# A chunked attention state, computed by heads right behind y

## The chip, the cores and the metric

The kernel runs on one core of one Trainium2 chip. The metric is the device time of one execution in microseconds (us), as the median of several runs.

## The reference

A recurrent attention with decay feeds a two-layer network:

```python
B, H, S, D = 4, 8, 768, 64
gamma = 1.0 - 2.0 ** (-5.0 - np.arange(H))
for t in range(S):
    state = gamma[None, :, None, None] * state + np.einsum('bhd,bhe->bhde', k[:, :, t], v[:, :, t])
    y[:, :, t] = scale * np.einsum('bhd,bhde->bhe', q[:, :, t], state)

x = y.transpose(0, 2, 1, 3).reshape(3072, 512)
h = x @ w_in                                   # 512 -> 2048
g = 0.5 * h * (1.0 + np.tanh(c * (h + 0.044715 * h * h * h)))
out = g @ w_out                                # 2048 -> 512
```

Inputs and output are float32. The kernel works in float16 with float32 sums.

## The kernel before, in words

The sequence is cut into six chunks of 128 positions; a chunk holds all four batches `b` and eight heads. A head has 64 dimensions, so heads go in four pairs `hp`, and `j` (0 or 1) is the head in its pair.

For each chunk `c` and batch `b` the attention has these steps. q and k are scaled by powers of gamma and cast to float16 (`prep1` and `prep_blk`, on GpSimd from chunk 2 on, L195 and L206), and their transposed form is made (for chunks 2 to 5 by DVE, `tr`, L263). `mm_A` (L273) multiplies k and q within the chunk, and DVE masks the product on its way out of PSUM (`ev_A`, L286). `mm_yc` (L295) multiplies the state of the earlier chunks with q, four matmuls of 128 columns; `mm_yi` (L308) adds the masked product times v, eight matmuls, each of one head: 64 weight columns, whose result goes to one half of the output partitions. `ev_Y` casts y to float16 as `xT`, the input of the network. Last, `mm_s` (L327) forms S, the sum over the chunk of k times v: four matmuls, one for each pair of heads, of 128 weight columns and 128 moving columns. Such a product holds the 64x64 blocks of the two heads on its diagonal and two mixed blocks that nothing reads. `ev_S` (L344) has DVE add the diagonal blocks to the decayed state `stg` into `st`, and `decay` (L353) has GpSimd scale `st` into `stg` for the next chunk.

The network runs on TensorE for each chunk: `moe1` (L434) with w_in, 16 blocks of hidden units, ScalarE's gelu (L449), then `moe2` (L479) with w_out, for each batch 16 matmuls of 512 columns in four units of four.

The order on every engine is the order of the program text; there is no scheduler. `run(units, after)` calls the units one by one and after unit `i` the attention steps listed for it. So the attention of chunk c+1 stands between the matmuls of the network of chunk c. For chunk 2 this is a run over the 16 `moe2` units of chunk 1: A behind units 3 and 7, y behind unit 11 (`att_Y`), and S of batch 0 to 3 behind units 12 to 15 (`att_S`: matmuls, DVE's adds, decay). Chunks 3, 4 and 5 have the same list, moved by 15 in a run of 16 `moe1` and 16 `moe2` units.

PSUM has eight banks in three pools: "h" and "o" with two each and "att" with four, taken in turn. A batch's A takes two banks of "att", y of batches 2 and 3 one each, and each S one.

Loads of q and k for chunks 2 to 5 in a blocked layout (L110), and of k and v (L98), go through SyncE's queue; v of chunk 2 alone is loaded and cast by GpSimd's queue (L670), in this kernel as in the changed one. Outputs go out mostly by GpSimd's queue (L506).

Of the kernel before, what the change touches and what calls it, by code (L numbers as in the profile page):

```python
# [12 lines left out]
ALU = mybir.AluOpType  # L13
# [3 lines left out]
def kernel(  # L17
# [9 lines left out]
    nc = tc.nc  # L27
    B, H, S, Dh = q.shape
    C = 128
    NCk = S // C  # L30
    NHP = H // 2
# [26 lines left out]
    att = ctx.enter_context(tc.tile_pool(name="att", bufs=4))  # L58
    xp = ctx.enter_context(tc.tile_pool(name="xp", bufs=2))
    gp = ctx.enter_context(tc.tile_pool(name="gp", bufs=2))  # L60
    op = ctx.enter_context(tc.tile_pool(name="op", bufs=4))
# [81 lines left out]
    for j in range(2):  # L143
# [3 lines left out]
        out=iden,  # L147
# [8 lines left out]
        out=mask.rearrange("p j hp t -> p (j hp) t"),  # L156
# [8 lines left out]
        out=misc[:, 0:1], in_=zero[:, 0:1], func=AF.Gelu_apprx_tanh, scale=1.0  # L165
# [10 lines left out]
    st = const.tile([128, NHP, B, 128], F16, name="st")  # L176
    nc.vector.memset(st, 0.0)
    stg = const.tile([128, NHP, B, 128], F32, name="stg")

    h16 = {}  # L180
# [39 lines left out]
    pss = {}  # L220
# [11 lines left out]
    def bank(tag, dt=F32, shape=(128, NHP, 128), name="ps"):  # L232
        return psum.tile(list(shape), dt, tag=tag, bufs=BANKS[tag], name=name)
# [24 lines left out]
    def ev_T(c, b, eng=nc.vector):  # L258
        copy_on(eng, qkT_tile(c, b), pss.pop(("T", c, b)))
# [29 lines left out]
    def mm_yc(c, b, tag):  # L289
        y_ps = pss["Y", c, b] = bank(tag, name="y_ps")  # L290
        if c == 0:
            return

        for hp in range(NHP):
            nc.tensor.matmul(  # L295
                out=y_ps[:, hp],
                lhsT=st[:, hp, b],
                rhs=qkT[c, b][:, 0, hp],
                start=(hp == 0),
                stop=False,  # L300
                skip_group_check=True,
            )

    def mm_yi(c, b):
        y_ps = pss["Y", c, b]
        for hp in range(NHP):
            for j in range(2):
                nc.tensor.matmul(  # L308
                    out=y_ps[j * 64:(j + 1) * 64, hp],
                    lhsT=h16["v", c, b][:, 2 * hp + j],  # L310
                    rhs=a_sb[c, b, j][:, hp],
                    start=(c == 0),
                    stop=True,
                    skip_group_check=True,
                )

    def ev_Y(c, b, eng=nc.vector):
        if c not in xT:
            xT[c] = xp.tile([128, NHP, B * C], F16, tag="x", name="xT")
        copy_on(eng, xT[c][:, :, b * C:(b + 1) * C], pss.pop(("Y", c, b)))  # L320

    def mm_s(c, b, tag="att"):
        if c + 1 >= NCk:
            return
        s_ps = pss["S", c, b] = bank(tag, name="s_ps")
        for hp in range(NHP):
            nc.tensor.matmul(  # L327
                out=s_ps[:, hp],
                lhsT=pair(h16["k", c, b], hp),
                rhs=pair(h16["v", c, b], hp),  # L330
                start=True,
                stop=True,
            )

    def ev_S(c, b, eng=nc.vector):
        if c + 1 >= NCk:
            return
        s_ps = pss.pop(("S", c, b))
        for j in range(2):
            sl = slice(j * 64, (j + 1) * 64)  # L340
            if c == 0:
                copy_on(eng, st[sl, :, b, sl], s_ps[sl, :, sl])
            else:
                eng.tensor_tensor(  # L344
                    out=st[sl, :, b, sl],
                    in0=s_ps[sl, :, sl],
                    in1=stg[sl, :, b, sl],
                    op=ALU.add,
                )

    def decay(c, b):
        if c + 2 < NCk:
            nc.gpsimd.tensor_tensor(  # L353
                out=stg[:, :, b],
                in0=st[:, :, b],
                in1=cst[:, OG:OG + NHP].unsqueeze(2).broadcast_to([128, NHP, 128]),
                op=ALU.mult,
            )

    def att_T(c, *bs):  # L360
        for b in bs:
            mm_T(c, b)
            ev_T(c, b)

    def att_S(c, b, tag="att"):
        mm_s(c, b, tag)
        ev_S(c, b)
        decay(c, b)

    def att_Y(c):  # L370

        tags = ("h", "h", "att", "att")
        for b in range(B):
            mm_yc(c, b, tags[b])
        for b in range(B):
            mm_yi(c, b)
        for b in range(B):
            ev_Y(c, b, (AC, VE)[b % 2])

# [71 lines left out]
    def moe1(c, fc):  # L451
        h_ps = bank("h", shape=(128, B * C), name="h_ps")
        moe1_mm(c, fc, h_ps, 0, B * C)
        gelu(g_tile(c, fc)[:, fc % 2], h_ps)
# [65 lines left out]
    def run(units, after):  # L520
        for i, u in enumerate(units):
            u()
            for f, *args in after.get(i, ()):
                f(*args)
# [99 lines left out]
    def units2(c, b, n=4, tag="o"):  # L624
        u = [(lambda i=i: moe2(c, b, range(i, i + n), tag)) for i in range(0, NF, n)]
        last = u[-1]
        u[-1] = lambda: (last(), ev_O(c, b))
        return u
# [6 lines left out]
    for nm, b in (  # L635
# [10 lines left out]
            12: [(prep1, AC, "v", 1, 1), (att_T, 1, 1), (preps, 1, 2)],  # L646
            13: [(att_AY, 1, (0,), "h", 1, (1,), AC)],
            14: [(prep1, AC, "v", 1, 2), (att_T, 1, 2), (preps, 1, 3), (att_S, 1, 0)],
            15: [
                (att_AY, 1, (1,), "h", 1, (2,), AC),  # L650
                (att_T, 1, 3),
                (att_S, 1, 1),
            ],
        },
# [20 lines left out]
    def prep(c, nms):  # L675

        for nm in nms:
# [10 lines left out]
            0: [(prep1, AC, "v", 1, 3)],  # L688
            1: [(att_AY, 1, (2,), "o", 1, (3,), VE)],
            3: [(att_S, 1, 2)],  # L690
            4: [(att_AY, 1, (3,), "o", 1, (), VE)],
            6: [(att_S, 1, 3)],
# [9 lines left out]
            3: [(att_AY, 2, (), "att", 2, (0, 1), None), (tr, 2, "k", 2, 3)],  # L702
            7: [(att_AY, 2, (), "att", 2, (2, 3), None)],
            11: [(att_Y, 2)],
            12: [(att_S, 2, 0)],
            13: [(att_S, 2, 1)],
            14: [(att_S, 2, 2)],
            15: [(att_S, 2, 3)],
        },
    )  # L710

# [1 line left out]
    for c in range(2, NCk - 1):  # L713
        n = c + 1
        after = {
            2: [(prep, n, "QKvk"), (tr, n, "q")],
            9: [(load, n + 1)] if n + 1 < NCk else [],
            15: [(tr, n, "k", 0, 1)],
            18: [(att_AY, n, (), "att", n, (0, 1), None), (tr, n, "k", 2, 3)],
            22: [(att_AY, n, (), "att", n, (2, 3), None)],  # L720
            26: [(att_Y, n)],
            27: [(att_S, n, 0)],
            28: [(att_S, n, 1)],
            29: [(att_S, n, 2)],
            30: [(att_S, n, 3)],
        }
        run(
            [(lambda fc=fc: moe1(c, fc)) for fc in range(NF)]
            + [x for b in range(B) for x in units2(c, b)],
            after,  # L730
        )
    c = NCk - 1
# [36 lines left out]
```

## Time and profile before

| | |
|---|---|
| median of 3 runs | 213.95 us (213.19 to 214.13) |
| profiled execution | 214.13 us, its span in the profile 212.0 us |
| granted TensorE clock | 1.0 of full speed |
| TensorE matmuls (PE) | busy 205.3 us, 97% of the span |
| weight loads (PEld), beside the matmuls | 110.7 us, 52% |
| GpSimd (POOL) | 102.5 us, 48% |
| VectorE (DVE) | 91.9 us, 43% |
| ScalarE (ACT) | 83.6 us, 39% |
| S matmuls, L327 | 80 in all, of 128x128x128; 48 of them in chunks 2 to 4 |
| y matmuls by heads, L308 | 192 in all, 128x64 weights, 128 columns |

The profile is of one execution. The span runs from the first to the last instruction; the execution's own time is 2.1 us longer. A matmul's duration in the profile reaches from its start to the end of its result, and matmuls overlap, so what a matmul costs is read from the distance between starts and not from its duration. The chain that ended last is followed back from the last instruction, at each step to what released it or to the instruction before it on its engine.

### The profile page before, as it was taken

To read this page: it belongs to the slowest core of one execution; us is meant where nothing else is said; L and a number is where in the kernel's file an instruction comes from. 1 tells how busy PE (TensorE), PEld (TensorE's weight loads), DVE (VectorE), ACT (ScalarE), POOL (GpSimd) and SP (SyncE) were. 2 spreads that over 40 slices of the span, in tenths; PEclk is the share of its full clock that TensorE was granted. 3 is DMA by queue.
4 is the path that set the end of the run, shared out by engine and by line. 5 is a ranking of instruction groups with operands and counts; after the bars stand their busy time and mean duration, and the time that the engine had idled before them with its cause. 6 is when DMAs were issued, how large, how long until landed. Compare 5 with 4: busy or idle time off the path is not lost.

```text
span 212.0 us, 3857 instructions
## 1 busy us (share of the span) xinstructions
PE 205.3 (97%) x1502; PEld 110.7 (52%) x1502; DVE 91.9 (43%) x163; ACT 83.6 (39%) x142; POOL 102.5 (48%) x123
## 2 busy tenths in 40 slices
PE   7998999999999899999999999999999999999993
PEld 2456444557897346544456444456444455444452
DVE  5697100198633775450866542566560562100001
ACT  2283662145465113466113366113366113466120
POOL 2597500314369756772876959461496711100100
PEclk9999999999999999999999999999999999999999
DMA  7999999997869998978999989797898021100112
GB/s 160 288 234 172 206 204 207 272 223 128 159 101 151 218 193 198 188 112 151 254 167 200 199 157 257 141 190 148 184 229 189 3 101 49 53 0 0 49 53 97
DMA packets 132690, 33.31 MB, mean 157 GB/s; under 512 B 126528, under 2 KB 130880, under 8 KB 132672
## 3 DMA queue, kind: packets, MB, share of 16 engines
q1 hardware_dynamic: 111088, 20.22, 49.8%
q0 software_dynamic: 9856, 9.44, 22.1%
q10 hardware_dynamic: 11728, 3.41, 7.0%
q8 instruction: 11, 0.18, 0.3%
q14 instruction: 7, 0.06, 0.1%
HBM read 31.48 MB, written 6.29 MB: 178 GB/s over the span
## 4 chain that ended last, share of the span: by engine, by line
PE 77%; DMA 9%; SPq 8%; POOL 2%; issue 1%; DVE 1%; POOLq 0%; DVEq 0%
PE o_ps L479 37%; PE h_ps L434 32%; SPq L110 8%; DMA k<-in_k_dram 5%; DMA w_in<-in_moe_w_in_dram 3%; PE a_ps L273 2%; PE y_ps L308 2%; PE y_ps L295 2%; PE s_ps L327 1%; DMA kT<-in_k_dram 1%; POOL kT L206 1%; POOL v L670 1%; POOL k L195 1%; PE qkT_ps L239 0%; DVE qkT L263 0%
## 5 line engine op out<-in xcount | busy, mean ns | idle before, releaser
L479 PE MATMUL o_ps<-w_out,g 128*128 128x512 f16 (+1 forms) x400 | 88.6, 371 | 0.0
L434 PE MATMUL h_ps<-xT,w_in 128*128 128x512 f16 (+1 forms) x464 | 85.1, 342 | 1.0 <-DMA w_in<-in_moe_w_in_dram 1.0
L449 ACT ACTIVATE g<-h_ps 128x512 f16<-128x512 f32 x96 | 56.9, 597 | 48.0 <-PE h_ps L434 47.9
L434 PEld LDWEIGHTS <-w_in 128*128 128x128 f16 x464 | 45.0, 98 | 38.7 <-DMA w_in<-in_moe_w_in_dram 1.2
L479 PEld LDWEIGHTS <-g 128*128 128x128 f16 x400 | 37.4, 98 | 38.6
L286 DVE TENSOR_TENSOR a_sb<-a_ps,mask 128x512 f16<-128x512 f32 x48 | 30.2, 684 | 17.1 <-PE a_ps L273 17.0
L195 POOL TENSOR_TENSOR k<-k,cst 128x512 f16<-128x512 f32 x23 | 23.7, 1052 | 16.4 <-DMA k<-in_k_dram 16.4
L501 ACT COPY o_sb<-o_ps 128x512 f32<-128x512 f32 x19 | 11.1, 586 | 51.8 <-PE o_ps L479 41.8
L506 POOL DMA_DIRECT2D out_dram<-o_sb x18 | 10.1, 564 | 40.3 <-ACT o_sb L501 33.4
L353 POOL TENSOR_TENSOR stg<-st,cst 128x512 f32<-128x512 f16 x16 | 16.4, 1041 | 8.9 <-DVE st L344 6.2
L206 POOL TENSOR_TENSOR kT<-kT,cst 128x512 f16<-128x512 f32 x16 | 16.3, 1055 | 7.7 <-DMA kT<-in_k_dram 7.7
L263 DVE STREAM_TRANSPOSE qkT<-q 128x512 f16<-128x512 f16 x16 | 11.4, 712 | 13.4 <-POOL q L206 13.4
L206 POOL TENSOR_TENSOR q<-q,cst 128x512 f16<-128x512 f32 x16 | 16.3, 1049 | 1.4 <-DMA kT<-in_k_dram 1.4
L263 DVE STREAM_TRANSPOSE qkT<-kT 128x512 f16<-128x512 f16 x16 | 10.9, 699 | 13.8 <-POOL kT L206 13.8
L344 DVE TENSOR_TENSOR st<-s_ps,stg 64x256 f16<-64x256 f32 x32 | 13.5, 422 | 5.0 <-PE s_ps L327 4.4
L195 DVE TENSOR_TENSOR q<-q,cst 128x512 f16<-128x512 f32 x8 | 6.3, 784 | 16.4 <-DMA q<-in_q_dram 16.4
L226 DVE CAST xT<-y_ps 128x512 f16<-128x512 f32 x11 | 7.2, 687 | 12.9 <-PE y_ps L308 12.9
L517 DVE COPY o_sb<-o_ps 128x256 f32<-128x256 f32 x2 | 0.9, 426 | 26.5 <-PE o_ps L479 26.5
L224 ACT CAST xT<-y_ps 128x512 f16<-128x512 f32 x13 | 7.2, 588 | 12.0 <-PE y_ps L308 11.9
L171 PE MATMUL spin_ps<-zero 128*128 128x512 f16 x30 | 10.4, 493 | 1.3 <-DVE zero L139 1.3
L192 POOL CAST v<-v 128x512 f16<-128x512 f32 x12 | 7.2, 613 | 6.8 <-DMA v<-in_v_dram 5.3
L273 PE MATMUL a_ps<-qkT 64*128 64x128 f16 x192 | 8.3, 218 | 1.0 <-DVE qkT L263 0.8
(40 smaller groups left out, 92.7 us busy)
## 6 DMA issues: line engine op xcount, KB each, us to landing
k<-in_k_dram SPq DMA_DIRECT2D x20, 256.0 KB, 4.4
out_dram<-o_sb POOLq DMA_DIRECT2D x18, 256.0 KB, 2.9
v<-in_v_dram SPq DMA_DIRECT2D x17, 256.0 KB, 4.4
q<-in_q_dram SPq DMA_DIRECT2D x64, 64.0 KB, 2.9
kT<-in_k_dram SPq DMA_DIRECT2D x64, 64.0 KB, 2.8
w_out<-in_moe_w_out_dram POOLq DMA_DIRECT2D x4, 512.0 KB, 16.2
q<-in_q_dram ACTq DMA_DIRECT2D x4, 256.0 KB, 8.0
k<-in_k_dram ACTq DMA_DIRECT2D x4, 256.0 KB, 7.7
```

The source lines that it names most:

```text
L110: nc.sync.dma_start(out=t[p0:p0 + 32, :, a, :], in_=src[j, dd, t0:t0 + 32])
L195: eng.tensor_tensor(out=t, in0=src, in1=cst[:, col:col + H].unsqueeze(2).broadcast_to([128, H, Dh]), op=ALU.mult,)
L206: nc.gpsimd.tensor_tensor(out=t, in0=ld_all((key, c))[:, b * NHP:(b + 1) * NHP].rearrange("p hp a d -> p (hp a) d"), in1=cst[:, col:col + ...
L263: nc.vector.transpose(out=qkT_tile(c, b)[:, "qk".index(nm)].rearrange("p hp t -> p (hp t)"), in_=blk16.pop((nm, c, b)).rearrange("p ha d - ...
L273: nc.tensor.matmul(out=ps[j][:, hp], lhsT=t[j * 64:(j + 1) * 64, 1, hp], rhs=t[j * 64:(j + 1) * 64, 0, hp], start=True, stop=True,)
L286: nc.vector.tensor_tensor(out=s, in0=ps[j], in1=mask[:, j], op=ALU.mult)
L344: eng.tensor_tensor(out=st[sl, :, b, sl], in0=s_ps[sl, :, sl], in1=stg[sl, :, b, sl], op=ALU.add,)
L353: nc.gpsimd.tensor_tensor(out=stg[:, :, b], in0=st[:, :, b], in1=cst[:, OG:OG + NHP].unsqueeze(2).broadcast_to([128, NHP, 128]), op=ALU.mult,)
L434: nc.tensor.matmul(out=out, lhsT=w_in_of(fc, kc), rhs=xT[c][:, kc, t0:t1], start=(kc == 0 and first), stop=(kc == NHP - 1), skip_group_che ...
L449: nc.scalar.activation(out=out, in_=in_, func=AF.Gelu_apprx_tanh, scale=1.0)
L479: nc.tensor.matmul(out=ps[:, n0:n1], lhsT=g_sb[c, fc // 2][:, fc % 2, b * C:(b + 1) * C], rhs=w_out_sb[fc // (NF // NO)][:, fc % (NF // NO ...
L501: nc.scalar.copy(out=o_sb, in_=ps)
```

## The change

S of chunks 2, 3 and 4 is computed head by head instead of pair by pair. In place of four matmuls of 128x128 weights and 128 columns for a batch there are eight, each with 64 columns of k as weights and 64 columns of v moving, whose results go to the lower and the upper half of the output partitions in turn. The results of two batches share one bank, so a chunk takes two banks of "att" and not four. All 32 matmuls of a chunk stand together behind the last y matmul, inside `att_Y`, and no longer one batch at a time behind units 12 to 15 of `moe2`. DVE's adds and GpSimd's decay stay behind these units (`ev_S2`). The list of the runs changes accordingly. Chunks 0 and 1 keep `att_S`.

```diff
+    def att_S2(c):
+
+        if c + 1 >= NCk:
+            return
+        for b in range(0, B, 2):
+            s_ps = bank("att", shape=(128, 2, NHP, 64), name="s_ps")
+            for i in range(2):
+                for hp in range(NHP):
+                    for j in range(2):
+                        nc.tensor.matmul(
+                            out=s_ps[j * 64:(j + 1) * 64, i, hp],
+                            lhsT=h16["k", c, b + i][:, 2 * hp + j],
+                            rhs=h16["v", c, b + i][:, 2 * hp + j],
+                            start=True,
+                            stop=True,
+                            skip_group_check=True,
+                        )
+            pss["S2", c, b] = s_ps
+
+    def ev_S2(c, b):
+        if c + 1 >= NCk:
+            return
+        s_ps = pss["S2", c, b // 2 * 2]
+        for j in range(2):
+            sl = slice(j * 64, (j + 1) * 64)
+            nc.vector.tensor_tensor(
+                out=st[sl, :, b, sl],
+                in0=s_ps[sl, b % 2],
+                in1=stg[sl, :, b, sl],
+                op=ALU.add,
+            )
+        decay(c, b)
+
     def att_S(c, b, tag="att"):
         mm_s(c, b, tag)
         ev_S(c, b)
...
         for b in range(B):
             mm_yi(c, b)
+        att_S2(c)
         for b in range(B):
             ev_Y(c, b, (AC, VE)[b % 2])
...
             11: [(att_Y, 2)],
-            12: [(att_S, 2, 0)],
-            13: [(att_S, 2, 1)],
-            14: [(att_S, 2, 2)],
-            15: [(att_S, 2, 3)],
+            12: [(ev_S2, 2, 0)],
+            13: [(ev_S2, 2, 1)],
+            14: [(ev_S2, 2, 2)],
+            15: [(ev_S2, 2, 3)],
...
             26: [(att_Y, n)],
-            27: [(att_S, n, 0)],
-            28: [(att_S, n, 1)],
-            29: [(att_S, n, 2)],
-            30: [(att_S, n, 3)],
+            27: [(ev_S2, n, 0)],
+            28: [(ev_S2, n, 1)],
+            29: [(ev_S2, n, 2)],
+            30: [(ev_S2, n, 3)],
```

## The prediction

> **What bounds the kernel now.** I read the page's busy line and its chain that ended last first, to learn which engine sets the end.
>
> ```profile
> PE 205.3 (97%) x1502; PEld 110.7 (52%) x1502; DVE 91.9 (43%) x163; ACT 83.6 (39%) x142; POOL 102.5 (48%) x123
> ...
> PE 77%; DMA 9%; SPq 8%; POOL 2%; issue 1%; DVE 1%; POOLq 0%; DVEq 0%
> PE o_ps L479 37%; PE h_ps L434 32%; SPq L110 8%; DMA k<-in_k_dram 5%; DMA w_in<-in_moe_w_in_dram 3%; PE a_ps L273 2%; PE y_ps L308 2%; PE y_ps L295 2%; PE s_ps L327 1%; DMA kT<-in_k_dram 1%; POOL kT L206 1%; POOL v L670 1%; POOL k L195 1%; PE qkT_ps L239 0%; DVE qkT L263 0%
> ```
>
> TensorE sets the end; no other engine passes 48%. The S matmuls (L327), which the change replaces, are on the chain themselves. Next the chain in order of time (start, length, what), around the change in chunk 2 and where chunk 3's attention begins:
>
> ```profile
> 79.89 0.89 PE y_ps L295 x16
> 80.78 1.01 PE y_ps L308 x32
> 81.79 0.97 PE o_ps L479 x4
> 82.76 0.22 PE s_ps L327 x4
> 82.99 0.86 PE o_ps L479 x4
> ...
> 86.25 13.81 PE h_ps L434 x64
> 100.06 2.59 PE o_ps L479 x12
> 102.65 0.55 PE a_ps L273 x16
> ```
>
> From 71.82 us to 208.59 us the chain is TensorE alone, piece against piece. So a nanosecond of TensorE saved at 82 us reaches the end, unless an operand is then late. The four S of a chunk appear as four pieces of 0.22 us between pieces of `moe2` (0.86 us).
>
> Third, TensorE's timeline at the same place (start, length until the last one ends, count). A piece's length less one matmul's own 0.22 us (219 ns in its group), over the steps between, is the step.
>
> ```profile
> 79.72 1.06 PE L295 MATMUL y_ps<-qkT,st 128*128 128x128 f16 x16
> 80.71 1.08 PE L308 MATMUL y_ps<-a_sb,v 128*64 128x128 f16 x32
> 81.73 1.04 PE L479 MATMUL o_ps<-w_out,g 128*128 128x512 f16 x4
> 82.60 0.39 PE L327 MATMUL s_ps<-v,k 128*128 128x128 f16 x4
> ```
>
> L295: (1.06-0.22)/15 = 56 ns a step for 128 columns. L308: 32 matmuls of half the width, two heads on the two halves of the output partitions: (1.08-0.22)/15 = 57 ns for a **pair**. So the two halves run beside each other, and a pair costs what one full matmul costs. L327: (0.39-0.22)/3 = 57 ns, one full matmul.
>
> **The change part by part.**
>
> *Removed:* 4 S of 4 matmuls in each of chunks 2, 3 and 4: 48 matmuls with 128 moving columns. By the chain 0.89/16 = 55.6 ns each: 48 x 55.6 = 2.67 us, all on the path. (Check: L479's groups of four around an S start at 81.73 and 82.82, 1.09 us apart; four of 13.81/64 = 215.8 ns are 0.86; the rest is 0.22.) What it computed beyond need was the off-diagonal half of each 128x128 product.
>
> *Added:* 96 matmuls with 64 moving columns and 64 weight columns in 48 pairs, laid out like L308 and right behind it. No row shows a matmul of 64 columns. Rows give the step at 512 columns (215.8 ns) and at 128 (55.6): slope 160.2/384 = 0.417 ns a column, rest 2.2 ns. For 64 columns: 26.7 + 2.2 = 28.9 ns a pair, if the halves run beside each other as in L308. 48 x 28.9 = 1.39 us. **Difference: 1.39 - 2.67 = -1.28 us**, -0.43 in each chunk.
>
> *Bounds of that price.* Three things could hold a pair above 28.9 ns. The weight loads: L308 loads 64 columns a matmul, and two narrow windows of its first loads show
>
> ```profile
> 80.71 0.11 PEld L308 LDWEIGHTS <-v 128*64 128x64 f16 x2
> ...
> 80.71 0.14 PEld L308 LDWEIGHTS <-v 128*64 128x64 f16 x4
> ```
>
> The first pair of loads takes 0.11 us to finish, the first two pairs 0.14: the second pair began 0.03 us behind the first. A load therefore occupies its half for some 0.03 us and not for the 0.11 that it lasts; that fits inside a 28.9 ns step with nothing to spare. Second, a step that doesn't shrink with the columns: at 56 ns a pair as in L308, the 48 pairs cost 2.69 us and nothing is gained. Third, the supply of instructions: the densest stretch of the trace is L295 with L308, 48 matmuls and 48 loads in 1.85 us (79.72 to the last start at 81.57), 19.3 ns an instruction. If that were a limit, 64 instructions of a chunk's S would take 1.24 us against 0.89: +1.04 us in all. On the other side, 26.7 ns with no rest gives -1.39. So the price lies between -1.39 and +1.04; I take -1.28, because the step follows the columns in both rows, and because L308's pairs, the second half of the dense stretch, still step as L295 does: nothing starves there.
>
> The Trainium skill speaks against the change at this point. "TensorE: Matmul & The Clock Gate", section on LDWEIGHTS, puts a load at columns over 1.2 ns, an estimated 53 ns for 64, and its section on weight-path modes gives the fast load to 128-column weights alone; by that a pair is held at 53 ns and the gain would be an estimated 0.1 us. The rows say 0.03 us, so I follow them. "TensorEngine Tiling (Array Packing)", section Instruction Overhead, says that a matmul has about 60 cycles of overhead and that a factor should not be taken from a dimension already small; by the first page's 2.4 GHz this is an estimated 25 ns, and counted for each of 96 matmuls one after another it would leave a gain of about 0.3 us. No row here is short enough to show it.
>
> *Moved:* S leaves its places behind units 12 to 15 of `moe2` and goes behind the y matmuls. The switch from half-width to full matmuls (L308 to L479: 0.97 in place of 0.86) stays one per chunk. S now uses two banks of the pool "att" in place of four; they are those in which chunk c's last A stood, which y has already waited for: no new wait. The order on DVE and POOL stays, and so does all that is issued by SP, ACT and POOL, transfers included. DVE's eight adds (0.42 us each, L344) and POOL's decay behind them can begin about 1 us earlier; what they write is read by the next chunk's y and adds, over 20 us later: nothing gained, nothing lost. If that cover were gone, the adds would cost 3.4 us a chunk.
>
> *What is late next.* Three margins shrink. POOL, DVE and POOL again:
>
> ```profile
> 80.12 1.04 POOL L195 TENSOR_TENSOR k<-k,cst 128x512 f16<-128x512 f32 x1 [0.85 <-DMA k<-in_k_dram]
> ...
> 101.58 0.71 DVE L263 STREAM_TRANSPOSE qkT<-kT 128x512 f16<-128x512 f16 x1 [0.30 <-POOL kT L206]
> ...
> 107.78 4.06 POOL L195 TENSOR_TENSOR k<-k,cst 128x512 f16<-128x512 f32 x4
> ```
>
> Chunk 2's k of batch 3 is ready at 81.16. Its S stood at 86.02, a margin of 4.9 us; now y's last pair starts at 81.57, S follows at 81.63 and reaches batch 3 after 12 pairs, at 81.98: margin 0.8. Chunk 3's is ready at 111.84 and wanted at about 112.5: 0.7. Chunk 3's A of batch 1 needs the transpose that ends at 102.29; A starts at 102.65 and its second batch 0.28 later, now all 0.43 earlier, so at 102.50: margin 0.2. If that transfer were 0.6 us later, the first 0.43 would be lost there. All three hold in this execution, so each costs nothing.
>
> **Sum.** Profiled execution 214.13 us (span 212.0): -1.28 gives 212.85. The median of the runs lies 0.18 lower: 213.95 - 1.28 = **212.7 us**, -0.6%.
>
> **The rivals.**
>
> *The pair doesn't get shorter* (chance 0.24). Loads, or a floor of each instruction, hold it near L308's 57 ns. For it: no row below 128 columns, and loads that just fit. Against it: the 0.03 us above. Time 213.3 to 214.0, which counts as no change.
>
> *Starved TensorE* (0.06): the 19.3 ns an instruction is a limit: 215.0.
>
> *k of chunk 2 comes too late* (0.08), the one that ends slower. These four loads landed late, beside the casting transfers of v:
>
> ```profile
> DMA to landing us min/median/max: 6.0/7.9/8.5
> ```
>
> Batch 3's took the 6.0 (issued at 74.04). With 8.5 it lands at 82.5 and is ready at 83.65: TensorE, with all `moe2` queued behind, stands 1.7 us: 214.3. With 10.2, the longest of any k load in the trace, it stands 3.4 us: 216.1, slower by 1.0%. It begins to count at 0.8 us late, eats the gain at 2.1, and is slower by over 0.5% at 3.2. Against it: loads and TensorE's position in this stage hang on the same queue, so they slip together.
>
> *The change doesn't do what it says:* the load of v by GpSimd's queue is already in the kernel before; only S is new. The instruction order of the changed kernel has the 96 matmuls of 64x64 behind y, so this rival gets nothing.
>
> **How the numbers follow.** Forecast 0.62, rivals 0.24, 0.06 and 0.08. 0.5%, about what a measurement of this kernel can tell, is 1.07 us: 212.88 is the border, and the forecast lies 0.2 beyond it. The three runs spread over 0.94 us, so I give three quarters of the forecast to faster: 0.47. Most of the late k and half of the starved case are slower: 0.08. The rest, 0.45, is the same. The range 212.2 to 214.3: below, the bound of -1.39 (212.56) less 0.4 of spread; above, no gain (213.95) and the late k at 8.5; the slower ends are the part left out. The forecast's own range is 212.2 to 213.2.
>
> **What would show it.** Right: in the chain one piece of S per chunk of about 0.47 us (16 pairs), steps of 29 ns a pair in TensorE's timeline, and `moe2` at 0.86 us a unit with nothing between; TensorE's chain still unbroken after 72 us. Wrong: a piece near 0.9 us (pairs at 56 ns, or 28 a matmul); steps that grow towards the end of a piece (supply); a wait of TensorE for POOL k L195 in chunk 2 or 3, or for DVE's transposes at 102 us.

## The result, and the profile after

The first four runs of the changed kernel have a median of 211.93 us (211.80 to 212.03), against 213.86 us before (213.19 to 214.13): ratio 0.9914, 95% interval 0.989 to 0.9938. The profiled execution took 211.80 us, its span 209.8 us. Later runs, below, put the change nearer to 1.2 us than to these 1.9.

The page after, busy line and chain:

```profile
PE 203.2 (97%) x1550; PEld 109.4 (52%) x1550; DVE 92.2 (44%) x163; ACT 83.8 (40%) x142; POOL 102.5 (49%) x123
...
PE 80%; SPq 9%; DMA 4%; POOL 3%; DVE 1%; issue 1%; POOLq 0%; DVEq 0%
```

TensorE still sets the end, with 48 matmuls more and 2.1 us less of busy time. The chain after in order of time (start, length, what), at the place shown of before:

```profile
78.84 0.89 PE y_ps L295 x16
79.74 1.01 PE y_ps L308 x32
80.75 0.51 PE s_ps L374 x32
81.25 3.56 PE o_ps L513 x16
84.81 13.81 PE h_ps L468 x64
98.63 2.59 PE o_ps L513 x12
101.22 0.55 PE a_ps L273 x16
```

S is one piece of 0.51 us in place of four of 0.22, and the four units of `moe2` behind it run through. TensorE's timeline there:

```profile
79.67 1.08 PE L308 MATMUL y_ps<-a_sb,v 128*64 128x128 f16 x32
80.58 0.67 PE L374 MATMUL s_ps<-v,k 128*64 128x64 f16 x32
81.19 0.60 PE L513 MATMUL o_ps<-w_out,g 128*128 128x512 f16 x2
```

One S matmul lasts 0.196 us, so a pair (one matmul for each half of the output partitions) takes (0.67-0.196)/15 = 31.6 ns; some expectations below round it to 31.7. The prediction had 28.9.

Where did the time go? The chain from chunk 2's second A to the last copy, before and after (first and last pieces):

```profile
71.82 0.40 PE a_ps L273 x8
...
208.62 0.43 DVE o_sb L517
```

```profile
70.77 0.40 PE a_ps L273 x8
...
206.40 0.42 DVE o_sb L551
```

From there to the start of the last copy 136.80 us became 135.63: **-1.17 us**, three times 0.39. The two profiles differ by 2.22 us in all (208.62 against 206.40); the other 1.05 us were gone before the first changed instruction, where both programs are the same. TensorE's timeline of before, near the start (`spin_ps` are matmuls on zeros that fill idle time):

```profile
4.22 3.03 PE L171 MATMUL spin_ps<-zero 128*128 128x512 f16 x7
...
19.20 1.05 PE L434 MATMUL h_ps<-xT,w_in 128*128 128x256 f16 x8 [1.01 <-DMA w_in<-in_moe_w_in_dram]
```

and after:

```profile
4.22 1.89 PE L171 MATMUL spin_ps<-zero 128*128 128x512 f16 x7
...
17.61 2.58 PE L468 MATMUL h_ps<-xT,w_in 128*128 128x256 f16 x22
```

The same seven of these filling matmuls took 3.03 us in one execution and 1.89 in the other, and w_in came in time in one and 1.0 us late in the other. Whether this belongs to the change was the first thing to test.

### The profile page after: what moved, and what is told of

It is laid out like the page before. It is cut to its first block, busy times and chain, and to the rows that moved or that the text cites. A ratio compares the mean times of both kernels' runs of the same rounds, so it can differ in the third digit from the quotient of the medians.

```text
span 209.8 us, 3948 instructions
## 1 busy us (share of the span) xinstructions
PE 203.2 (97%) x1550; PEld 109.4 (52%) x1550; DVE 92.2 (44%) x163; ACT 83.8 (40%) x142; POOL 102.5 (49%) x123
## 4 chain that ended last, share of the span: by engine, by line
PE 80%; SPq 9%; DMA 4%; POOL 3%; DVE 1%; issue 1%; POOLq 0%; DVEq 0%
PE o_ps L513 37%; PE h_ps L468 33%; SPq L110 8%; DMA k<-in_k_dram 3%; PE a_ps L273 3%; PE y_ps L308 2%; PE y_ps L295 2%; DMA kT<-in_k_dram 1%; POOL kT L206 1%; POOL v L704 1%; POOL k L195 1%; PE s_ps L374 1%; PE spin_ps L171 1%; PE s_ps L327 1%; SPq L98 1%
## 5 line engine op out<-in xcount | busy, mean ns | idle before, releaser
L513 PE MATMUL o_ps<-w_out,g 128*128 128x512 f16 (+1 forms) x400 | 86.8, 371 | 0.0
L513 PEld LDWEIGHTS <-g 128*128 128x128 f16 x400 | 37.9, 98 | 41.0
L195 DVE TENSOR_TENSOR q<-q,cst 128x512 f16<-128x512 f32 x8 | 6.8, 851 | 17.4 <-DMA q<-in_q_dram 17.4
L171 PE MATMUL spin_ps<-zero 128*128 128x512 f16 x30 | 9.3, 446 | 1.3 <-DVE zero L139 1.3
L390 DVE TENSOR_TENSOR st<-s_ps,stg 64x256 f16<-64x256 f32 x24 | 10.1, 421 | 0.7
```

Of the source, the lines that this page charges most:

```text
L171: nc.tensor.matmul(out=ps, lhsT=zero[:, 0:128], rhs=zero, start=True, stop=True)
L195: eng.tensor_tensor(out=t, in0=src, in1=cst[:, col:col + H].unsqueeze(2).broadcast_to([128, H, Dh]), op=ALU.mult,)
L513: nc.tensor.matmul(out=ps[:, n0:n1], lhsT=g_sb[c, fc // 2][:, fc % 2, b * C:(b + 1) * C], rhs=w_out_sb[fc // (NF // NO)][:, fc % (NF // NO ...
```

## The experiments

| kernel | median us (runs) | ratio to before, 95% interval | chunk 2's second A at, us | from there to the end, us |
|---|---|---|---|---|
| before | 213.86 (4) | 1 | 71.82 | 136.80 |
| changed | 211.93 (4) | 0.9914 (0.989 to 0.9938) | 70.77 | 135.63 |
| e1_null | 214.03 (12) | 0.9998 (0.9972 to 1.0024) | 70.97 | 136.94 |
| e2_again | 212.75 (12) | 0.9932 (0.9893 to 0.9971) | 72.04 | 137.32 |
| e9_after3 | 212.25 (12) | 0.9958 (0.9924 to 0.9993) | 70.82 | 135.64 |
| e12_after4 | 213.23 (12) | 0.9977 (0.9943 to 1.0011) | 70.52 | 136.42 |
| e3_chunk4 | 213.83 (12) | 1.001 (0.9978 to 1.0043) | 70.92 | 136.52 |
| e4_twice | 214.35 (12) | 1.0029 (0.9998 to 1.0061) | 70.96 | 137.94 |
| e5_old_place | 214.71 (12) | 1.0044 (1.001 to 1.0079) | 70.58 | 138.34 |
| e6_full | 215.37 (12) | 1.0037 (1.0003 to 1.007) | 70.90 | 137.97 |
| e7_v_later | 212.25 (12) | 0.9931 (0.9901 to 0.9961) | | |
| e8_n32 | 214.65 (1) | | 72.06 | 137.11 |
| e10_single | 216.82 (1) | | 71.70 | 139.72 |
| e11_v_early | 215.32 (12) | 1.0043 (1.0 to 1.0085) | 73.69 | 136.74 |

The last two columns are one profiled execution each. e7_v_later moves its wait behind this point, and so has no comparable stretch. Ratios are estimated from all runs of a comparison and are not the quotients of the medians (they differ by up to 0.4%). They are to runs of before on the same chip, whose medians were 213.84 (e1 to e4), 213.53 (e5, e7, e8, e9) and 213.81 (e6, e10, e11, e12).

**e1_null: is the start the change's?**

```diff
+    def att_S2(c): ...        # defined, never called
+    def ev_S2(c, b): ...      # defined, never called
```

> The kernel before, with the new functions defined and never called: the same instructions. Theory A (the change is worth three times 0.39 us, and the rest of the 1.9 us between the medians is the start of the execution, which differs from run to run): ratio 1.000, but single runs of this kernel and of the one before spread over about 1 us, and the profile reaches chunk 2's A anywhere from 70.8 to 71.9 us. Theory B (the changed kernel's first 70 us are faster by 0.8 us always, because of where its program lies): ratio 1.000 too, but with runs near 213.9 and chunk 2's A at about 71.8.

Ratio 0.9998, and the 12 runs spread from 212.97 to 216.93 us. The chain of this kernel's profile:

```profile
70.97 0.40 PE a_ps L273 x8
...
207.91 0.42 DVE o_sb L550
```

The same instructions as before reach chunk 2's second A 0.85 us earlier than in the profile of before, and 0.2 us from the changed kernel's. So the early part varies by itself. What went wrong there in the profile of before is the late w_in: of all the profiles here it alone shows TensorE waiting for w_in (1.0 us), while the slow filling matmuls cost little at this point: in e1_null all 13 of them took 5.47 us, against 5.59 before and 4.45 in the changed kernel.

**e2_again, e9_after3, e12_after4: the changed kernel, unchanged, three times.**

> The changed kernel, unchanged. Theory A: over more runs beside the kernel before on one chip the difference settles nearer to -1.2 us (ratio 0.9945, 212.7 where before is 213.9), with runs that spread like those of before; A of chunk 2 to the last instruction stays 135.6 us. Theory B: -1.9 us again (ratio 0.991), runs within 0.3 us.

> The changed kernel once more, for its spread. Theory A (the change is worth 1.17 us, the sum of three chunks read from the traces, and the front of the execution varies from run to run): median 212.4 to 213.0 and a ratio near 0.9945. Theory B (a lasting 0.8 us more): median near 211.9, ratio 0.991.

> The changed kernel beside the one before it, to compare on the same chip. If the change is worth the 1.17 us of the traces: ratio 0.9945, its interval holding this value. If it is worth 1.9 us as in the first four runs: 0.991.

The medians lie 1.09, 1.28 and 0.58 us under those of before. All 40 runs of the changed kernel have a median of 212.68 us, the 97 runs of before beside them 213.81: 1.13 us. The intervals of all three hold the 1.17 us of the traces (0.9945), and those of the second and third leave out the first 0.9914, while the third's also holds 1: theory A. The single runs spread from 211.55 to 217.17 us. Only 7 of the 36 later ones lie at or under 212.03 us, where all of the first four lay. That is more than chance among like runs would often give; what those four had in common isn't on record.

A part of the 1.13 us lies outside the span of the profile: 11 of the 93 runs of before in these three comparisons took 2.5 to 3.7 us beyond their span, all 40 runs of the changed kernel 2.0 to 2.1. By the spans alone the medians of these 93 runs and the 36 of the changed kernel are 211.6 and 210.7 us, 0.9 apart. Why is not shown.

The profiles say where runs lose time. In e12_after4, TensorE's timeline at chunk 3's A:

```profile
100.91 0.40 PE L273 MATMUL a_ps<-qkT 64*128 64x128 f16 x8
101.91 0.40 PE L273 MATMUL a_ps<-qkT 64*128 64x128 f16 x8 [0.61 <-DVE qkT L263]
```

Its stretch of 136.42 us is 0.79 longer than the changed kernel's first. The transpose of kT for batch 1 ended at 101.85 us, 0.56 later than in the changed kernel's first profile; TensorE began A 0.2 us earlier than there and had to wait. This is the margin that the prediction put at 0.2 us. In e2_again the wait came at chunk 2's A, 1.6 and 0.6 us long, and then the chain has

```profile
72.04 0.40 PE a_ps L273 x8
72.44 5.25 PE o_ps L513 x16
```

where every other profile of the changed kernel has 3.56 for these 16 matmuls. The windows (start and end, length, busy times of PE, PEld, DVE, ACT, POOL, then granted clock, DMA share, GB/s) tell why, first e2_again, then the changed kernel's first profile:

```profile
72.00:78.00 6.00, 5.96 (x38) 2.52 (x40) 3.70 (x6) 0.28 (x1) 4.24 (x5) 0.72 1.28 223
```

```profile
71.00:77.00 6.00, 6.00 (x48) 2.78 (x42) 5.35 (x10) 0.59 (x1) 2.01 (x2) 1.00 1.46 186
```

The granted clock fell to a mean of 0.72 after the wait: 1.69 us more, which is the whole excess of this stretch (137.32 against 135.63). Much of the spread looks like this: the 7 of the 36 later runs with a mean granted clock of 0.992 or less took 214.45 us or more, the other 29 at most 213.94.

**e3_chunk4: a third of the change.**

```diff
+        if c == 4:
+            att_S2(c)
...
-            27: [(ev_S2, n, 0)],
+            27: [(ev_S2 if n == 4 else att_S, n, 0)],
```

> Only chunk 4's S is computed by columns right behind y; chunks 2 and 3 as before. The program up to 140 us is that of before. Theory A: -0.39 us (ratio 0.998). Theory B, that the start depends on the program as a whole: -0.39 and, if this program too falls on the fast side, up to -0.76 more (ratio 0.9945).

The ratio's interval holds 1 and 0.998 and decides nothing. The trace does: from chunk 4's first A (133.71 us) to the last copy (207.44) are 73.73 us, against 74.12 before (134.50 to 208.62) and 73.72 in the changed kernel (132.68 to 206.40). One chunk is worth 0.39 us.

**e4_twice: are 32 pairs on end as cheap as 16?**

```diff
-            for i in range(2):
+            for i in (0, 1, 0, 1):
```

> The changed kernel with each of the 96 matmuls of S issued twice, the second time over the same bank: 48 more pairs. If a pair costs the 31.7 ns seen in the changed kernel's trace, the piece per chunk grows from 0.51 to 1.01 us and the time by 1.5 us over the changed kernel. If TensorE is starved when half-width matmuls go on for longer, the later pairs take more than 31.7 ns and the growth is over 2 us. By the prediction's 28.9 ns: 1.39.

The chain:

```profile
112.83 1.01 PE s_ps L374 x64
```

1.01 us for 32 pairs, 31.6 ns each, as for 16. The median lies 1.60 us over e2_again on the same chip; 3 x 0.50 = 1.5 were expected. (The stretch is 2.31 us longer than the changed kernel's first; the other 0.8 are a wait at chunk 3's A, as in e12_after4.) TensorE isn't starved in a burst twice as long.

**e5_old_place: narrow, but not behind y.**

```diff
-    def att_S2(c):
+    def att_S2(c, *bs):
...
-        for b in range(0, B, 2):
+        for b in bs:
...
-            for i in range(2):
+            for i in range(1):
...
-        s_ps = pss["S2", c, b // 2 * 2]
+        att_S2(c, b)
+        s_ps = pss["S2", c, b]
...
-                in0=s_ps[sl, b % 2],
+                in0=s_ps[sl, 0],
...
-        att_S2(c)
```

> S of chunks 2 to 4 by columns as in the changed kernel, but left in the old place, one batch at a time behind units 12 to 15 of moe2, a bank each. If the gain needs the place (each entry into half-width matmuls and each return costs some 0.1 us, as before and behind y), a batch costs 4 pairs of 31.7 ns and two switches, 0.13 + 0.20 = 0.33 us against 0.22: +1.2 us over before, ratio 1.006. If the narrower matmuls alone make the gain and the switches are hidden behind moe2: 12 x (0.13 - 0.22) = -1.1 us, ratio 0.995.

```profile
80.56 0.97 PE o_ps L513 x4
81.53 0.24 PE s_ps L374 x8
81.78 0.97 PE o_ps L513 x4
```

A batch takes 0.24 us for its four pairs, and each unit of `moe2` behind half-width matmuls 0.97 in place of 0.86: 1.22 us from the start of one unit to the next, against 1.09 before. 12 x 0.13 = 1.6 us, close to the 1.54 of the stretch (138.34 against 136.80); by the medians 1.18 us. Narrow matmuls lose by themselves; they gain here only where the step in and out of half-width is already paid by y.

**e6_full: behind y, but not narrow.**

```diff
         for b in range(B):
             mm_yi(c, b)
+        if c + 1 < NCk:
+            mm_s(c, 0)
+            mm_s(c, 1)
         for b in range(B):
             ev_Y(c, b, (AC, VE)[b % 2])
+        if c + 1 < NCk:
+            mm_s(c, 2)
+            mm_s(c, 3)
...
-            12: [(att_S, 2, 0)],
+            12: [(ev_Sd, 2, 0)],                                    # adds and decay alone
...
```

> The place alone: the old full-width S matmuls, four for each batch and a bank each, all put behind the last y matmul. Batches 2 and 3 then take the banks in which y of batches 2 and 3 stands. If the place alone gains something (fewer interruptions of moe2), the ratio to before is below 0.998. If full-width S costs the same 0.22 us a batch anywhere, and TensorE must wait for the two casts of y before it can write there: 0.3 to 0.6 us more per chunk, +0.9 to +1.8 us over before, and a wait of TensorE for ACT or DVE xT in the profile.

```profile
79.86 0.59 PE y_ps L308 x16
...
80.54 1.30 DVE xT L226 x2
81.88 0.38 PE s_ps L327 x4
```

The chain leaves TensorE for DVE's casts of y: the last S waits for the bank in which y of batch 3 stands. The stretch is 1.17 us longer than before, 0.39 a chunk, and the median 1.56 us. So the place alone loses too. In the changed kernel two batches share a bank, S needs no bank in which y stands, and its chain shows no such wait.

**e8_n32 and e10_single: what holds a pair at 31.6 ns?**

```diff
...
-                            rhs=h16["v", c, b + i][:, 2 * hp + j],
+                            rhs=h16["v", c, b + i][:, 2 * hp + j, e:e + 32],   # e = 0, 32
...
```

Both kernels have this: each matmul of S becomes two of 32 moving columns, and each loads its weights. In e8_n32 the halves still alternate; in e10_single the 8 matmuls of the lower half come before the 8 of the upper.

> The changed kernel with every matmul of S cut into two of 32 moving columns, weights loaded again for each: 32 pairs per chunk in place of 16. If the 31.7 ns of a pair with 64 columns is set by the weight loads (64 columns each), a pair stays at 31 to 32 ns and the piece grows from 0.51 to about 1.0 us a chunk, +1.5 us in all. If it is set by the moving columns, a pair takes 16 to 20 ns and the piece stays at 0.5 to 0.65 us. If a floor per instruction sets it (4 instructions in 31.7 ns, 8 ns each), 31.7 too, and then the distance between a pair's load and the next load tells load from floor.

> As the run with 32 moving columns (64 matmuls of S per chunk), but not in pairs: for each bank and batch first the 8 matmuls of the lower half, then the 8 of the upper half. If the 31.7 ns is the weight load of one half, the loads no longer run beside each other: 64 x 31.7 = 2.0 us a chunk, +3.0 us over the paired run. If it is a floor of the instructions (about 8 ns each), it doesn't matter which half they go to: 1.0 us a chunk as in the paired run.

TensorE's timeline of e8_n32, then of e10_single:

```profile
81.87 1.16 PE L374 MATMUL s_ps<-v,k 128*64 128x32 f16 x64
```

```profile
83.20 1.47 PE L374 MATMUL s_ps<-v,k 128*64 128x32 f16 x64
```

With half the moving columns a pair still takes (1.16-0.18)/31 = 31.6 ns. So at 64 columns it is not the columns that bind, but what a pair has in common in both: its two weight loads, or its four instructions. Unpaired, a matmul takes (1.47-0.18)/63 = 20 ns, between the 16 of a floor per instruction and the 32 of one load after another. A plain floor of 8 ns an instruction doesn't fit, since the order mattered; loads that never overlap don't fit either. The last five matmuls of the same piece, which by the program's order all belong to the upper half, show what a half does when the other has nothing left:

```profile
84.36 0.31 PE L374 MATMUL s_ps<-v,k 128*64 128x32 f16 x5
```

(0.31-0.18)/4 = 32 ns each. In the middle of the piece starts come mostly 5 to 6 and 26 to 27 ns apart in turn, and the program's 16th matmul, known by its semaphore, is the 19th to start. So a half takes some 32 ns for a matmul with its load, and the other half's matmuls begin ahead of their turn beside it. Whether it is the load or the matmul that holds a half at 32 ns stays open, since every matmul here has its own load. For the load speaks that in before's y the second load on a half starts 0.03 us behind the first, while the matmuls that use them start 0.08 us apart (80.71 and 80.79).

**e7_v_later and e11_v_early: can the wait at chunk 2's A go?**

```diff
-            7: [(prep, 2, "Q"), (load_v16, 2)],
+            7: [(prep, 2, "Q")],                                               # e7, e11
...
-            10: [(prep, 2, "Kk")],                                             # e7
+            9: [(prep_blk, "k", 2, 0), (prep_blk, "k", 2, 1), (load_v16, 2)],   # e7
+            10: [(prep_blk, "k", 2, 2), (prep_blk, "k", 2, 3), (prep, 2, "k")], # e7
...
+            5: [(load_v16, 2)],                                                # e11
```

> The changed kernel with GpSimd's four issues of v of chunk 2 (3.6 us on its queue) moved behind the scaling of kT of batches 0 and 1. In all profiles so far TensorE stands at chunk 2's A, about 1 us beyond its usual step, for the transposes that follow this scaling; GpSimd's queue is full ahead of it. If that queue sets this moment, the wait goes and the kernel gains 0.8 to 1.0 us over the changed one (ratio to before 0.990). If kT's landing sets it, at 65 to 66 us, the gain is under 0.3 us; if v or kT of batches 2 and 3 now come late at the next A or at y, TensorE waits there instead and nothing is gained.

> The changed kernel with the four issues of v of chunk 2 moved ahead on GpSimd's queue, to the 2.5 us in which it stands idle before the last decay of chunk 1. The wait of TensorE at chunk 2's A should shrink from about 1.0 us to what kT's landing leaves. If the queue sets this moment: -0.5 to -1.0 us from the changed kernel (ratio to before about 0.990 to 0.992). If v's transfers, now beside those of q and kT, delay kT's landing by as much, nothing is gained, and the wait stays under another releaser.

e7_v_later on GpSimd, and on TensorE:

```profile
68.84 3.57 POOL L704 DMA_DIRECT2D v<-in_v_dram  x4
72.39 2.09 POOL L206 TENSOR_TENSOR kT<-kT,cst 128x512 f16<-128x512 f32 x2
```

```profile
74.28 0.40 PE L273 MATMUL a_ps<-qkT 64*128 64x128 f16 x8 [0.63 <-DVE qkT L263]
75.29 0.40 PE L273 MATMUL a_ps<-qkT 64*128 64x128 f16 x8 [0.61 <-DVE qkT L263]
```

The wait moved from batches 0 and 1 to batches 2 and 3, whose kT now stood behind the four issues. The median is the same as that of e9_after3 on the same chip, 212.25 us; only its runs lie closer together (211.82 to 212.94, against 211.55 to 214.62). e11_v_early is slower (215.32 us, against 213.23 of e12_after4 on the same chip):

```profile
70.84 4.07 POOL L206 TENSOR_TENSOR kT<-kT,cst 128x512 f16<-128x512 f32 x4 [5.87 <-DMA out_dram<-o_sb]
```

GpSimd stood 5.9 us before kT, by the profile for a transfer (an output's, on the queue that also carries kT), and TensorE 3.6 and 0.4 us behind it. The queue's time was gained and lost again to the transfers; that v's four, now ahead, are what slowed them is argued, not shown. No version here is shown to be faster than the changed kernel.

## Why the prediction was right or wrong

*The time.* 211.93 us lay 0.27 us below the range. The step that failed is the low end of the range: the bound of the price less 0.4 us of spread. I took the early 70 us as common to both and the spread from three runs. In the two profiles the early parts differ by 1.05 us, and e1_null, 0.85 us ahead of before without the change, shows that this is not the change's; the 40 runs of the changed kernel spread over 5.6 us. Over more runs the medians were 212.75, 212.25 and 213.23 us, and 212.68 over all, beside the predicted 212.7. That closeness is partly luck: the start of the sum, 213.95, was 0.14 above the 213.81 of 97 runs, and the gain of 1.28 was 0.15 above the 1.13 of the medians.

*The bound.* Right: from 72 us on the chain is TensorE, and what was saved there reached the end, 3 x 0.39 us.

*Removed and added.* The removed 2.67 us were right. Of the added 1.39, the step of a pair was mis-sized: 31.6 ns, not 28.9, so 48 pairs cost 1.52 us. The line through 512 and 128 columns doesn't reach down to 64; e8_n32 shows the same 31.6 ns at 32 columns. The sum is then -1.15 in place of -1.28, and the traces show -1.17. The bound by the weight loads came close to this: it put a load at "some 0.03 us", inside 28.9 ns with nothing to spare, and a half in fact takes 32 ns.

*The rivals.* That the pair doesn't get shorter had the right mechanism in weight loads or an instruction floor, but at 32 ns and not at 56. The 53 ns estimated for a 64-column load by the Trainium skill's rule ("TensorE: Matmul & The Clock Gate", section on LDWEIGHTS) are too long for this case: two such loads, one for each half, recur every 31.6 ns. Starvation is excluded by e4_twice.

*Place and banks.* Right, and now shown: narrow matmuls in the old place lose 1.5 us in the trace (e5_old_place), and full-width ones in the new place, a bank for each batch, 1.2 us (e6_full).

*What is late next.* The margins were the weak point. k of chunk 2, batch 3, had 0.8 us by my sum. GpSimd's timeline of the changed kernel (the last two k):

```profile
78.77 2.05 POOL L195 TENSOR_TENSOR k<-k,cst 128x512 f16<-128x512 f32 x2
```

It was ready at 80.82 us. The S of this batch began at about 80.58 + 12 x 0.032 = 80.96, and the load of its first weights, which are k, 0.03 us ahead: some 0.1 us to spare. No profile here shows TensorE waiting for it. The 0.2 us of chunk 3's transpose did give way, in e12_after4 and e4_twice, and cost 0.8 us each time.

## What to carry to other kernels

A product whose off-diagonal half is thrown away can be cut into half-width matmuls that run in pairs. In this kernel it paid only next to others of the same width, since each step in and out costs about 0.1 us, and with results that fit into free banks. Don't extrapolate the price of a matmul down in columns without a row that short: here a pair took 32 ns, whether 64 or 32 columns moved. Before comparing two kernels by a microsecond, compare the part of their traces that is the same in both; if that differs, only the stretch behind the change tells its size.

## What the runs showed of the hardware

- A pause of TensorE can cost more than its length. After waits of 1.6 and 0.6 us within 2.7 us (e2_again) the next 16 matmuls of 512 columns took 5.25 us in place of 3.56, at a mean granted clock of 0.72; e10_single, with 1.7 and 0.6 us, shows the same 5.25 and 0.72. In e11_v_early, with 3.6 and 0.4 us, the clock was at 0.90 in the stretch that holds the wait and at 0.77 behind it, and the 16 took 4.45. e8_n32, with 1.2 and 0.6 us, still has 3.56. The Trainium skill ("TensorE: Matmul & The Clock Gate", section on HAM oscillation, its name for the clock gate falling and rising again) names idle gaps of over some 3.4 us for this; here shorter ones were enough.
- Two halves of the array need not be fed strictly in turn: 8 matmuls of one half before 8 of the other took 20 ns each (e10_single), against 16 when alternating (e8_n32), because matmuls of the waiting half started before earlier ones of the program. A half left to itself took 32 ns for each.
